# Product of the softmax weights with V as two 64-row halves in two accumulator banks, in bursts of 256 columns, and score maxima 512 wide in a ring of three banks

## The chip, the cores and the metric

The kernel runs on one core of one Trainium2 chip. The metric is the device time of one execution in microseconds (us). The engines of the core work side by side, each through its own list of instructions in order: TensorE (PE in the profile, its weight loads are PEld), VectorE (DVE), ScalarE (ACT), GpSimd (POOL) and SyncE (SP), which here only issues DMAs. TensorE writes its results into PSUM, which has eight banks of 512 fp32 columns on 128 partitions.

## What is computed

```python
def reference(A_x, A_wqkv, A_wo, B_x, B_wqkv, B_wo, gate_w):
    # S = 2048 tokens, D = 512, H = 32 heads of Dh = 16, all fp32; A and B differ in their weights
    def mha(x, wqkv, wo):
        qkv = (x @ wqkv).reshape(B, S, 3, H, Dh).transpose(2, 0, 3, 1, 4)
        q, k, v = qkv[0], qkv[1], qkv[2]
        scores = jnp.einsum("bhqd,bhkd->bhqk", q, k) * (Dh ** -0.5)
        p = softmax(scores, axis=-1)
        o = jnp.einsum("bhqk,bhkd->bhqd", p, v)
        return o.transpose(0, 2, 1, 3).reshape(B, S, D) @ wo
    x = A_x
    g = sigmoid((x * gate_w).sum(-1, keepdims=True))
    return g * mha(x, A_wqkv, A_wo) + (1 - g) * mha(x, B_wqkv, B_wo)
```

There are 64 heads in all, 32 of each side, each with a 2048 by 2048 matrix of scores.

## The kernel before

**Stages.** A prologue computes q, k and v of both sides from the input and stores them in DRAM (`project_qk`, `project_v`); the main loop runs over 64 heads x 16 = 1024 *rounds*, two in each turn; an end finishes the last head and the last output rows. While the main loop runs, heads that are done are divided by their softmax sums and multiplied by `wo` (`load_den`, `invert_den`, `load_num`, `normalize`, `split_out`, `project_out`). Those steps hang on round numbers, in a table that `at(...)` fills.

**A head, three matmuls.** The row maxima are needed before the exponentials, so each score is computed twice. (1) `max_part` (L113) multiplies q by k for 128 queries and 512 keys into `ps_m`, and VectorE takes the maximum over the keys (L125). A tile of 128 queries has 2048 keys: parts 0 and 1 are 512 keys, each in one bank (`ps_m1`, two buffers), and part 2 is 1024 keys in two banks (`ps_m2`, one buffer), so a tile takes three reductions. (2) `score` (L573) multiplies k by q for 128 keys and 512 queries into `ps_st` (three buffers of one bank), with the maxima subtracted by two more contraction rows, and ScalarE takes the exponential into `p` (L585). (3) `attend` (L515) multiplies `p` by v and a column of ones, so that row 16 of 17 is the softmax sum, into the one bank `acc`. The four groups of 512 queries go to four column tiles of the TensorE array (`tile_position=(0, 32 * c)`), each with all 128 rows, and run side by side. `acc` adds over the 16 rounds of a head. Then ScalarE copies it out (L549, `ev`) and a DMA stores it in `od`.

**Rows of the array.** The maxima use 48 contraction rows and the scores 50, at row 0 or row 64 by turns (`rows()`), so two of them run side by side in two row halves with all 128 columns. `attend` uses 128 rows and 32-column tiles. `p` and v are fp32, and each such matmul leaves two records, two passes. The others are fp32r and take one.

**Order.** `tc.manual_schedule()` is on: each engine runs its instructions in the order in which the code issues them. For two rounds the string `FULL` sets it: `e` is a score matmul with its exponential, `m` a part of a maximum tile (`M` the double one), and a digit n is a burst of `attend` over n quarters of 128 query columns. The string is `e3eemm2eMeme3emeM`. Scores run about 2 rounds ahead of `attend`, and maxima 20 rounds ahead of the scores. A `project_out` goes out ahead of a burst. In the prologue `run_ahead` issues the first 20 tiles of maxima, three parts after each `project_v`.

**PSUM.** `ps_m1` two banks, `ps_m2` two, `ps_st` three, `acc` one. A result of `project_out` takes a `ps_m1` buffer.

Of the kernel before, what the change touches and what calls it, by code (L numbers as in the profile page):

```python
# [32 lines left out]
P = 128  # L33
S = 2048
DM = 512
# [16 lines left out]
def gated_mha(ctx: ExitStack, tc: tile.TileContext, xT, x, wqkv_a, wo_a, wqkv_b, wo_b, gate_w, out):  # L52
# [8 lines left out]
    ps_m1 = ctx.enter_context(tc.tile_pool(name="ps_m1", bufs=2, space=PSUM))  # L61
    ps_m2 = ctx.enter_context(tc.tile_pool(name="ps_m2", bufs=1, space=PSUM))
# [4 lines left out]
    od = [dram.tile([HG, NQ, 32, 512], F32, name=f"od{g}") for g in range(2 * NG)]  # L67
# [37 lines left out]
    PARTS = ((0,), (1,), (2, 3))  # L105
# [7 lines left out]
    def max_part(m, part):  # L113
        h, t = divmod(m, NT)
        if t == 0 and part == 0:
            mxp[h] = small.tile([P, NT, 3], F32, name="mxp")
        q, k = q_st[h % 3], k_st[h % 3]
        chunks = PARTS[part]
        n = len(chunks)
        ps = (ps_m1 if n == 1 else ps_m2).tile([P, n * 512], F32, name=f"ps_m{n}")  # L120
        for i, c in enumerate(chunks):
            b = rows()
            pe.matmul(ps[:, i * 512:(i + 1) * 512], q[b:b + SC, t * P:(t + 1) * P],  # L123
                      k[b:b + SC, c * 512:(c + 1) * 512], start=True, stop=True)
        dve.tensor_reduce(mxp[h][:, t, part:part + 1], ps, op=ALU.max, axis=AX.X)  # L125
# [35 lines left out]
    with tc.tile_pool(name="xs", bufs=1) as xs, tc.tile_pool(name="pro", bufs=2) as pro, \  # L161
# [59 lines left out]
        def project_v(s, t):  # L221
            hi, lo = wblocks[s, 2 * DM]
            c, o = divmod(t * P, 512)
            last = s == 1 and t == NT - 1
            ps = ps_m1.tile([P, 512], F32, name="ps_m1") if last else ps_pro.tile([P, 1024], F32, name="ps_pro")
            n = 0
            for a, b in ((xh[c], hi), (xl[c], hi), (xh[c], lo)):
                for k in range(KC):
                    pe.matmul(ps[:, :DM], a[:, k, o:o + P], b[:, k], start=n == 0, stop=n == 3 * KC - 1)  # L229
# [20 lines left out]
        ahead = [(m, part) for m in range(NT + LEAD) for part in range(3)]  # L250

        def run_ahead(n):
            turn[0] = 0
            for _ in range(n):
                m, part = ahead.pop(0)
                max_part(m, part)
                if (m, part) == (NT - 1, 2):
                    max_split(0)
                    pending.append(0)

        pending = []
        for i, (s, g, isk) in enumerate(blocks):
            block(split_w, i + 1)
            block(load_w, i + 3)
            if i in (2, 8):
                load_w(i // 8, 2 * DM, DM)
            if i in (4, 9):
                split_w(i // 8, 2 * DM, DM)
            project_qk(s, g, isk, lambda: run_ahead((i >= 10) + (i >= 13)))
# [27 lines left out]
    acc = ps_acc.tile([P, 512], F32, name="acc")  # L297
    dve.memset(acc, 0.0)
# [60 lines left out]
    def load_den(G):  # L359
        o, n = od[G], gh[G] * DH  # L360
        dens[G] = work.tile([P, P], F32, name="dn")
        nc.sync.dma_start(dens[G][:n], bass.AP(tensor=o.tensor, offset=o.offset + 16 * 512,
                                               ap=[[32 * 512, gh[G] * NQ], [P, 4], [1, P]]))

    def invert_den(G, i):
        n = gh[G] * DH
        if i == 0:
            dens["r", G] = work.tile([P, P], F32, name="rn")
        rn = dens["r", G]
        c = slice(i * 64, i * 64 + 64)  # L370
        dve.reciprocal(rn[:n, c], dens[G][:n, c])  # L371
        if i:
            nc.sync.dma_start(rd[G][:gh[G]].rearrange("h (x e) -> (h x) e", e=P), rn[:n])


    def load_num(G, c):
        o, r, n = od[G], rd[G], gh[G] * DH
        num = work.tile([P, 512], F32, name="o_num", bufs=4)
        rb = work.tile([P, 512], F32, name="rb", bufs=4)
        nc.sync.dma_start(num[:n], bass.AP(tensor=o.tensor, offset=o.offset + c * 32 * 512,  # L380
                                           ap=[[NQ * 32 * 512, gh[G]], [512, DH], [1, 512]]))
# [4 lines left out]
    def normalize(G, c):  # L386
        n = gh[G] * DH
        num, rb = nums[G, c]
        (dve if G == LAST else pool).tensor_tensor(num[:n], num[:n], rb[:n], op=ALU.mult)

    def split_out(G, c, slot):
        n = gh[G] * DH
        num, _ = nums.pop((G, c))
# [7 lines left out]
    def result_bank():  # L401
        banks.append(len(banks) % 5)
        if banks[-1] % 2 or not fill_only:
            return ps_m1.tile([P, 512], F32, name="ps_m1")
# [86 lines left out]
    for side in range(2):  # L491
# [4 lines left out]
        for c in range(NQ):  # L496
            for i, G in enumerate(groups):
                at(end + 22 + 16 * c + i, load_num, G, c)
                at(end + 28 + 16 * c + i, normalize, G, c)
                at(end + 34 + 16 * c + 2 * i, split_out, G, c, i)  # L500
            for i in range(4):
                at(end + 42 + 16 * c + 2 * i, project_out, side, 4 * c + i)
# [5 lines left out]
    for c in range(NQ):  # L508
        at(end + 4 + c // 2, load_num, LAST, c)
        at(end + 10 + c // 2, normalize, LAST, c)  # L510
        at(end + 11 + c // 2, split_out, LAST, c, c)
# [12 lines left out]
    def attend(r, qa, qb):  # L524
# [6 lines left out]
        for c in range(NQ):  # L531
            pe.matmul(acc[32 * c:32 * c + 17, qa * P:qb * P], v[:, 4 * a + c if final else kt, j],  # L532
                      p[:, c * 512 + qa * P:c * 512 + qb * P], start=first and qa == 0, stop=last,
                      tile_position=(0, 32 * c), skip_group_check=True)
# [3 lines left out]
        if final and last:  # L538
            ev = work.tile([P, 512], F32, name="ev")
            dve.tensor_copy(ev, acc)  # L540
# [5 lines left out]
        elif last:  # L546
            G, j = divmod(h, HG)
            ev = work.tile([P, 512], F32, name="ev")
            act.copy(ev, acc)  # L549
            nc.sync.dma_start(od[G][j].rearrange("c r t -> (c r) t"), ev)  # L550
# [15 lines left out]
    def score_bank(r):  # L566
        if r >= ROUNDS - NT - LEAD:
            late[0] += 1
            if late[0] % 6 in (1, 3):
                return ps_m1.tile([P, 512], F32, name="ps_m1")  # L570
            if late[0] % 6 == 5:
                return ps_m2.tile([P, 1024], F32, name="ps_m2")[:, :512]
# [17 lines left out]
    FULL = "e3eemm2eMeme3emeM"  # L590
    after = {}

    for r in range(0, ROUNDS, 2):
# [12 lines left out]
        for step in FULL if m < ROUNDS else ():  # L606
# [3 lines left out]
            elif step in "mM":  # L610
                max_part(m + parts // 3, parts % 3)
# [50 lines left out]
```

## Time and profile before

| | |
|---|---|
| time, two runs | 2849.75 and 2850.84 us, median 2850.3 us |
| profiled execution | span 2848.8 us from the first to the last instruction, granted TensorE clock 0.998; what lies around the span is 1.5 us of the median |
| TensorE busy | 2830.3 us, 99% |
| VectorE busy | 2559.5 us, 90% |
| ScalarE busy | 2260.3 us, 79% |
| GpSimd busy | 225.3 us, 8% |
| DMA | 214.65 MB, 75 GB/s on average |
| maxima reductions, L125 | 3072, 2419.6 us |
| exponentials, L585 | 4056 into `ps_st` tiles, 2157.0 us |

How to read it: matmuls are pipelined and the ends in the records are modelled, so a matmul of 0.4 us may be followed by the next one of its kind 0.23 us later, and a TensorE that is 99% busy is not at its limit for 99% of the time. Records of VectorE overlap in the same way when it works without a gap. What one instruction costs in a row of its kind is read from start to start.

### The profile page before, as it was taken

What the parts mean: (1) busy time and instruction counts of PE and PEld (TensorE: products, weight loads), DVE (VectorE), ACT (ScalarE), POOL (GpSimd) and SP (SyncE); (2) the same over time, 40 slices, a digit from 0 to 9 for tenths busy, and PEclk for the clock granted to TensorE, in tenths of its full rate; (3) what the DMA queues carried; (4) which work ended last, traced back from release to release, by engine and by line L of the source; (5) the groups of instructions that cost most, each with busy time, mean ns of one, the idle gap of its engine ahead of it and who ended that gap; (6) DMA issues with size and microseconds to landing.
All of it is one profiled execution on the core that took longest, in us unless ns stands there. A gap on an engine that the chain in (4) does not pass through costs nothing.

```text
span 2848.8 us, 62282 instructions
## 1 busy us (share of the span) xinstructions
PE 2830.3 (99%) x26016; PEld 1372.6 (48%) x26016; DVE 2559.5 (90%) x3371; ACT 2260.3 (79%) x4253; POOL 225.3 (8%) x369
## 2 busy tenths in 40 slices
PE   8999999999999999999999999999999999999999
PEld 7877444444444444444444455444444444444544
DVE  4135899999999999999999988999999999998894
ACT  3221788889888888988988866888888888987775
POOL 1000232000000000000100231000000000011201
PEclk9999999999999999999999999999999999999999
DMA  7673333222332222332322342232222233323302
GB/s 244 195 230 121 88 80 80 40 49 54 66 58 55 52 56 46 54 56 55 85 55 49 95 101 55 54 56 48 59 47 55 55 74 66 54 67 85 72 10 91
DMA packets 83759, 214.65 MB, mean 75 GB/s; under 512 B 21878, under 2 KB 32086, under 8 KB 70934
## 3 DMA queue, kind: packets, MB, share of 16 engines
q1 hardware_dynamic: 80918, 201.76, 31.1%
q0 software_dynamic: 2560, 8.91, 1.2%
q8 instruction: 205, 3.36, 0.5%
q14 instruction: 76, 0.62, 0.1%
HBM read 145.87 MB, written 64.74 MB: 74 GB/s over the span
## 4 chain that ended last, share of the span: by engine, by line
PE 91%; DVE 7%; DMA 1%; ACT 0%; SPq 0%; issue 0%; POOL 0%; DVEq 0%; ACTq 0%
PE acc L532 34%; PE ps_st L583 29%; PE ps_m L123 14%; DVE mxp L125 7%; PE ps_pro L206 6%; PE ps_m L416 3%; PE ps_pro L229 3%; DMA raw<-in_xT 0%; DMA rb<-rd 0%; PE ps_st L416 0%; DVE rn L371 0%; PE ps_st L467 0%; ACT p L585 0%; PE ps_m L583 0%; PE ps_m L467 0%
## 5 line engine op out<-in xcount | busy, mean ns | idle before, releaser
L125 DVE TENSOR_REDUCE mxp<-ps_m 128x1 f32<-128x512 f32 (+1 forms) x3072 | 2419.6, 861 | 49.8 <-PE ps_m L123 43.5
L585 ACT ACTIVATE p<-ps_st 128x512 f32<-128x512 f32 x4056 | 2157.0, 601 | 332.6 <-PE ps_st L583 233.7
L583 PE MATMUL ps_st<-q_st,k_st 50*128 50x512 f32 x4056 | 1322.9, 445 | 0.0
L123 PE MATMUL ps_m<-k_st,q_st 48*128 48x512 f32 x4096 | 1199.0, 434 | 3.6 <-DVE mxp L125 3.1
L532 PE MATMUL acc<-p,vg 128*17 128x384 f32 (+1 forms) x16208 | 1188.3, 386 | 3.0 <-DVE ev L540 2.0
L583 PEld LDWEIGHTS ps_st<-q_st,k_st 50*128 50x128 f32 x4056 | 591.8, 184 | 745.7 <-ACT p L585 723.8
L123 PEld LDWEIGHTS ps_m<-k_st,q_st 48*128 48x128 f32 x4096 | 543.1, 185 | 105.6 <-DVE mxp L125 39.4
L532 PEld LDWEIGHTS acc<-p,vg 128*17 128x17 f32 x16208 | 314.0, 96 | 512.1 <-issue 481.0
L136 POOL CAST mparts<-mrow 128x16 fp32r<-128x16 f32 x64 | 12.5, 196 | 2194.5 <-DVE mrow L135 2194.5
L211 DVE TENSOR_TENSOR part<-ps_pro,part 128x1024 fp32r<-128x1024 f32 x32 | 39.2, 1225 | 110.5 <-ACT part L210 110.5
L210 ACT CAST part<-ps_pro 128x1024 fp32r<-128x1024 f32 x32 | 32.5, 1015 | 132.0 <-PE ps_pro L206 132.0
L416 PE MATMUL ps_m<-wo,ot 128*128 128x512 f32 (+1 forms) x354 | 90.4, 400 | 0.0
L206 PE MATMUL ps_pro<-xh,whi 128*128 128x512 f32 x256 | 73.2, 405 | 8.0 <-ACT xh L192 7.5
L232 ACT COPY v_st<-ps_pro 128x512 f32<-128x512 f32 x31 | 18.2, 587 | 77.4 <-PE ps_pro L229 77.4
L416 PEld LDWEIGHTS ps_m<-wo,ot 128*128 128x128 f32 (+1 forms) x354 | 64.0, 188 | 23.8 <-DVE mxp L125 8.7
L206 PE MATMUL ps_pro<-xh,wlo 128*128 128x512 f32 x256 | 69.3, 393 | 0.0
L206 PE MATMUL ps_pro<-xl,whi 128*128 128x512 f32 x256 | 69.2, 393 | 0.0
L206 PEld LDWEIGHTS ps_pro<-xh,whi 128*128 128x128 f32 x256 | 47.9, 192 | 23.1 <-ACT xh L192 10.2
L206 PEld LDWEIGHTS ps_pro<-xh,wlo 128*128 128x128 f32 x256 | 48.6, 190 | 10.3
L206 PEld LDWEIGHTS ps_pro<-xl,whi 128*128 128x128 f32 x256 | 48.6, 190 | 10.2
L180 DVE TENSOR_TENSOR wlo<-wraw,whi 128x512 fp32r<-128x512 f32 x16 | 10.9, 684 | 46.8 <-ACT whi L179 46.8
L549 ACT COPY ev<-acc 128x512 f32<-128x512 f32 x63 | 38.2, 607 | 0.0
(92 smaller groups left out, 634.4 us busy)
## 6 DMA issues: line engine op xcount, KB each, us to landing
k_st<-kd SPq DMA_DIRECT2D x128, 256.0 KB
q_st<-qd SPq DMA_DIRECT2D x128, 256.0 KB
qd<-part SPq DMA_DIRECT2D x32, 512.0 KB
kd<-part SPq DMA_DIRECT2D x32, 512.0 KB
k_st<-kd SPq DMA_DIRECT2D x128, 128.0 KB
q_st<-qd SPq DMA_DIRECT2D x128, 128.0 KB
od<-ev SPq DMA_DIRECT2D x63, 256.0 KB
vd<-v_st SPq DMA_DIRECT2D x32, 272.0 KB
```

The lines of the kernel that those rows point to most:

```text
L123: pe.matmul(ps[:, i * 512:(i + 1) * 512], q[b:b + SC, t * P:(t + 1) * P], k[b:b + SC, c * 512:(c + 1) * 512], start=True, stop=True)
L125: dve.tensor_reduce(mxp[h][:, t, part:part + 1], ps, op=ALU.max, axis=AX.X)
L206: pe.matmul(ps[:, c * 512:(c + 1) * 512], a[:, k], b[:, k], start=n == 0, stop=n == 3 * KC - 1)
L210: act.copy(pt[0], ps)
L211: dve.tensor_tensor(pt[1], ps, pt[0].bitcast(F32), op=ALU.subtract)
L229: pe.matmul(ps[:, :DM], a[:, k, o:o + P], b[:, k], start=n == 0, stop=n == 3 * KC - 1)
L232: act.copy(v_st[t % 2][:, :, 0:16], v)
L416: pe.matmul(ps, ot[a][:n, slot, sl], wt[b][:n, g], start=G == groups[0] and i == 0, stop=G == groups[-1] and i == 2)
L532: pe.matmul(acc[32 * c:32 * c + 17, qa * P:qb * P], v[:, 4 * a + c if final else kt, j], p[:, c * 512 + qa * P:c * 512 + qb * P], start=fi ...
L549: act.copy(ev, acc)
L583: pe.matmul(ps, k[b:b + SC + 2, kk * P:(kk + 1) * P], q[b:b + SC + 2, cc * 512:(cc + 1) * 512], start=True, stop=True)
L585: act.activation(pt[r][:, c * 512:(c + 1) * 512], ps, AF.Exp, scale=SCALE)
```

## The change

- `attend` splits each matmul of 128 contraction rows into two of 64 rows (rows 0 to 63 and 64 to 127 of `p` and v), which go to the two row halves of the array and into two accumulator banks, `acc0` and `acc1`. A burst has eight matmuls where it had four.
- At the end of a head ScalarE copies both banks out, and two DMAs store them in two `od` tensors. The sum of the two halves is taken later, where the heads are divided: one more load and one more addition in `normalize` and `invert_den`, and for the last head one more VectorE addition.
- The second accumulator takes a bank from the maxima. `ps_m` is one ring of three banks, and a tile of maxima has four parts of 512 keys: four reductions where there were three.
- `FULL` is `2emem2emem2emem2emem`: four bursts of two quarters (256 columns) for two rounds where there were three of 3, 2 and 3 quarters. `run_ahead` issues four parts after each `project_v`. Results of `project_out` and some scores of the last head use the ring of three.
- The steps that divide and project are moved by some rounds in their table.

```diff
-    ps_m1 = ctx.enter_context(tc.tile_pool(name="ps_m1", bufs=2, space=PSUM))
-    ps_m2 = ctx.enter_context(tc.tile_pool(name="ps_m2", bufs=1, space=PSUM))
+    ps_m = ctx.enter_context(tc.tile_pool(name="ps_m", bufs=3, space=PSUM))
...
     def max_part(m, part):
...
-        chunks = PARTS[part]
-        n = len(chunks)
-        ps = (ps_m1 if n == 1 else ps_m2).tile([P, n * 512], F32, name=f"ps_m{n}")
-        for i, c in enumerate(chunks):
-            b = rows()
-            pe.matmul(ps[:, i * 512:(i + 1) * 512], q[b:b + SC, t * P:(t + 1) * P],
-                      k[b:b + SC, c * 512:(c + 1) * 512], start=True, stop=True)
+        ps = ps_m.tile([P, 512], F32, name="ps_m")
+        b = rows()
+        pe.matmul(ps, q[b:b + SC, t * P:(t + 1) * P], k[b:b + SC, part * 512:(part + 1) * 512],
+                  start=True, stop=True)
         dve.tensor_reduce(mxp[h][:, t, part:part + 1], ps, op=ALU.max, axis=AX.X)
...
             if t and t != NT - 2:
-                run_ahead(3)
+                run_ahead(4)
...
-    acc = ps_acc.tile([P, 512], F32, name="acc")
+    acc = [ps_acc.tile([P, 512], F32, name=f"acc{i}") for i in range(2)]
...
     def normalize(G, c):
-        num, rb = nums[G, c]
-        (dve if G == LAST else pool).tensor_tensor(num[:n], num[:n], rb[:n], op=ALU.mult)
+        (num, more), rb = nums[G, c]
+        eng = dve if G == LAST else pool
+        eng.tensor_tensor(num[:n], num[:n], more[:n], op=ALU.add)
+        eng.tensor_tensor(num[:n], num[:n], rb[:n], op=ALU.mult)
...
     def attend(r, qa, qb):
...
         for c in range(NQ):
-            pe.matmul(acc[32 * c:32 * c + 17, qa * P:qb * P], v[:, 4 * a + c if final else kt, j],
-                      p[:, c * 512 + qa * P:c * 512 + qb * P], start=first and qa == 0, stop=last,
-                      tile_position=(0, 32 * c), skip_group_check=True)
+            for i, b in enumerate(HALVES):
+                pe.matmul(acc[i][32 * c:32 * c + 17, qa * P:qb * P],
+                          v[b:b + 64, 4 * a + c if final else kt, j],
+                          p[b:b + 64, c * 512 + qa * P:c * 512 + qb * P], start=first and qa == 0, stop=last,
+                          tile_position=(b, 32 * c), skip_group_check=True)
...
         if final and last:
-            dve.tensor_copy(ev, acc)
+            dve.tensor_copy(ev, acc[0])
+            dve.tensor_tensor(ev, ev, acc[1], op=ALU.add)
...
         elif last:
-            act.copy(ev, acc)
-            nc.sync.dma_start(od[G][j].rearrange("c r t -> (c r) t"), ev)
+            for i in range(2):
+                ev = work.tile([P, 512], F32, name=f"ev{i}", bufs=1)
+                act.copy(ev, acc[i])
+                nc.sync.dma_start(od[G][i][j].rearrange("c r t -> (c r) t"), ev)
...
-    FULL = "e3eemm2eMeme3emeM"
+    FULL = "2emem2emem2emem2emem"
```

In the main loop TensorE's list reads so before, from one burst of 384 columns to the middle burst and beyond it (`ps_m1` and `ps_m2` are the buffers of maxima, `x4` are the four column tiles):

```order
L532 MATMUL acc_2015<-p_11674,vg_8358 17x384 x4
L583 MATMUL ps_st_11744<-q_st0_113,k_st0_114 128x512
L583 MATMUL ps_st_11747<-q_st0_113,k_st0_114 128x512
L123 MATMUL ps_m1_11750<-k_st1_118,q_st1_117 128x512
L123 MATMUL ps_m1_11753<-k_st1_118,q_st1_117 128x512
L532 MATMUL acc_2015<-p_11674,vg_8358 17x128 x4
L532 MATMUL acc_2015<-p_11709,vg_8358 17x128 x4
L583 MATMUL ps_st_11764<-q_st0_113,k_st0_114 128x512
```

The middle burst crosses from one round's `p` to the next, so its 256 columns are two groups of 128. In the changed kernel the list of the same loop, from the end of one burst to the start of the next, is:

```order
L534 MATMUL acc0_2060<-p_17319,vg_10345 17x256
L534 MATMUL acc1_2061<-p_17319,vg_10345 17x256
L586 MATMUL ps_st_17422<-q_st1_122,k_st1_123 128x512
L118 MATMUL ps_m_17425<-k_st2_2056,q_st2_2055 128x512
L586 MATMUL ps_st_17428<-q_st1_122,k_st1_123 128x512
L118 MATMUL ps_m_17431<-k_st2_2056,q_st2_2055 128x512
L534 MATMUL acc0_2060<-p_17360,vg_10345 17x256
L534 MATMUL acc1_2061<-p_17360,vg_10345 17x256
```

The last two rows are followed by three more pairs, one for each further column tile. Every burst now has eight matmuls in two banks, and between any two bursts stand two scores and two maxima.

In the prologue, TensorE's list around the maxima after one `project_v` (L229) was:

```order
L229 MATMUL ps_pro<-wvlo,xh_133 128x512 x4
L123 MATMUL ps_m_1631<-k_st_114,q_st_113 128x512
L123 MATMUL ps_m_1634<-k_st_114,q_st_113 128x512
L123 MATMUL ps_m_1637<-k_st_114,q_st_113 128x512 x2
L229 MATMUL ps_pro<-wvhi,xh_133 128x512 x4
```

and in the changed kernel, where `project_v` is L224:

```order
L224 MATMUL ps_pro<-wvlo,xh_138 128x512 x4
L118 MATMUL ps_m<-k_st_119,q_st_118 128x512 x4
L224 MATMUL ps_pro<-wvhi,xh_139 128x512 x4
L224 MATMUL ps_pro<-wvhi,xl_143 128x512 x4
L224 MATMUL ps_pro<-wvlo,xh_139 128x512 x4
```

The four maxima matmuls went into four banks, two of them as one buffer. Now they are four tiles of a ring of three.

On ScalarE the end of the first head reads so before (`ev` is the copy of the accumulator; the `x70` and `x64` are the exponentials):

```order
L232 COPY v_st_141<-ps_pro 128x32x16
L232 COPY v_st_142<-ps_m_1967 128x32x16
L585 ACTIVATE p<-ps_st 128x512 x70
L549 COPY ev<-acc 128x512
L585 ACTIVATE p<-ps_st 128x512 x64
```

and in the changed kernel:

```order
L227 COPY v_st_147<-ps_m 128x32x16
L588 ACTIVATE p<-ps_st 128x512 x70
L554 COPY ev_2810<-acc_2060 128x512
L554 COPY ev_2813<-acc_2061 128x512
L588 ACTIVATE p<-ps_st 128x512 x64
```

Two copies stand one behind the other between the same exponentials.

More of the change, by code (lines that the diff above doesn't have):

```diff
@@ L249, in gated_mha @@
                 block(load_w, c)
-        ahead = [(m, part) for m in range(NT + LEAD) for part in range(3)]
+        ahead = [(m, part) for m in range(NT + LEAD) for part in range(NQ)]
         def run_ahead(n):
@@ L568, in score_bank @@
             late[0] += 1
[L569 to L572, printed above, removed]
+            if late[0] % 2:
+                return ps_m.tile([P, 512], F32, name="ps_m")
         return ps_st.tile([P, 512], F32, name="ps_st")
```

62 lines of the change are left out of this document (32 added, 30 removed).

## The prediction

> **What bounds the kernel now.** The page's first part and its chain say TensorE:
>
> ```profile
> PE 2830.3 (99%) x26016; PEld 1372.6 (48%) x26016; DVE 2559.5 (90%) x3371; ACT 2260.3 (79%) x4253; POOL 225.3 (8%) x369
> PE 91%; DVE 7%; DMA 1%; ACT 0%; SPq 0%; issue 0%; POOL 0%; DVEq 0%; ACTq 0%
> ```
>
> But a busy TensorE is not one at its limit, so I read stages next: the table by stretches, first the long parts of the main loop, then one plain head and one in which output rows are projected.
>
> ```profile
> core 0: us, PE busy (x) PEld busy (x) DVE busy (x) ACT busy (x) POOL busy (x), PEclk, DMA share, GB/s
> 340.00:1600.00 1260.00, 1258.79 (x12678) 555.04 (x12680) 1255.90 (x1668) 1129.62 (x2148) 83.93 (x169) 1.00 0.31 60
> 1800.00:2560.00 760.00, 759.45 (x7657) 335.02 (x7660) 757.62 (x1005) 681.38 (x1295) 31.19 (x66) 1.00 0.29 57
> ...
> 836.90:875.00 38.10, 38.10 (x388) 16.85 (x385) 37.99 (x51) 34.29 (x67) 0.42 (x2) 1.00 0.28 52
> 875.00:913.00 38.00, 38.00 (x388) 16.82 (x384) 37.90 (x51) 34.18 (x67) 0.42 (x2) 1.00 0.27 51
> ...
> 1650.40:1700.00 49.60, 49.60 (x435) 25.55 (x432) 41.34 (x56) 34.28 (x67) 13.53 (x16) 1.00 0.35 87
> ```
>
> Over 2020 us of the main loop VectorE is busy for 1255.90 of 1260 and 757.62 of 760 us, 99.7%. A head takes 38.05 us there. Only with `project_out` does it idle (41.34 of 49.60 us), in 8 of the 64 heads. The waits agree: VectorE waits for maxima matmuls 48 times in all, while TensorE's waits for VectorE are short.
>
> ```profile
> DVE mxp L125 <- PE ps_m L123: 43.5, 48, 3.9
> PEld ps_m L123 <- DVE mxp L125: 39.4, 131, 0.9
> PEld acc L532 <- ACT ev L549: 23.6, 63, 1.2
> ```
>
> So **VectorE's reductions set the pace now**, with TensorE close behind. How close is read from single starts. Two rounds of TensorE:
>
> ```profile
> 1500.98 0.84 PE L532 MATMUL acc<-p,vg 128*17 128x384 f32 x8
> 1501.76 0.50 PE L583 MATMUL ps_st<-q_st,k_st 50*128 50x512 f32 x2
> 1502.09 0.39 PE L123 MATMUL ps_m<-k_st,q_st 48*128 48x512 f32 x2
> 1502.41 0.63 PE L532 MATMUL acc<-p,vg 128*17 128x128 f32 x16
> 1502.97 0.50 PE L583 MATMUL ps_st<-q_st,k_st 50*128 50x512 f32 x1
> ...
> 1503.87 0.84 PE L532 MATMUL acc<-p,vg 128*17 128x384 f32 x8
> 1504.64 0.50 PE L583 MATMUL ps_st<-q_st,k_st 50*128 50x512 f32 x1
> ...
> 1505.67 0.52 PE L532 MATMUL acc<-p,vg 128*17 128x384 f32 x4
> ```
>
> A burst of 384 columns holds TensorE 0.77 us until the next kind of matmul begins (1500.98 to 1501.76, 1503.87 to 1504.64), the middle burst of 256 columns 0.56. Two pairs of score and maximum take 0.65 (1501.76 to 1502.41), three pairs 0.90 (1502.97 to 1503.87). Without waits two rounds are 0.77 + 0.65 + 0.56 + 0.90 + 0.77 + 0.90 = 4.55 us; they take 4.69 here, the 0.13 more in the last stretch. VectorE in the same place:
>
> ```profile
> 1500.20 1.28 DVE L125 TENSOR_REDUCE mxp<-ps_m 128x1 f32<-128x512 f32 x2
> 1501.39 1.22 DVE L125 TENSOR_REDUCE mxp<-ps_m 128x1 f32<-128x1024 f32 x1
> 1501.39 1.81 DVE L125 TENSOR_REDUCE mxp<-ps_m 128x1 f32<-128x1024 f32 x2
> ```
>
> Two 512-wide reductions take 1.19 us from start to start of what follows (1500.20 to 1501.39). In the third row a wide one and a narrow one last 1.81; the second row of the pair 1500.20 gives a narrow one's own record as 1.28 - 0.60 = 0.68, so the wide one holds VectorE 1.81 - 0.68 = 1.13. A tile costs 1.19 + 1.13 = 2.32.
>
> **The change, part by part.** *Reductions.* Four narrow ones cost 2 x 1.19 = 2.38 per tile, 0.06 more: a wide reduction of 1024 columns pays its fixed part once. Nothing hides this on an engine that is 99.7% busy, so VectorE alone already needs 16 x 0.06 = 1.0 us more per head, about 39.05 us, if it waits no less than now.
>
> *Bursts.* The columns to stream stay the same; the number of bursts in two rounds goes from three to four. Each end of a burst costs something: 0.77 - 0.56 = 0.21 for 128 columns more in two passes is 0.82 ns per column and pass, so 256 columns stream in 0.42 and 0.14 of the 0.56 is switching. A further 0.15 lies in the stretch of pairs, where the first two take 0.65 and the third adds 0.25. Does switching stay when a burst uses the same row halves as the scores? The trace has no such burst. The nearest rows are a switch in columns alone, from `project_out` (128 rows and 128 columns) to a burst (128 rows, 32-column tiles):
>
> ```profile
> 1628.11 3.04 PE L416 MATMUL ps_m<-wo,ot 128*128 128x512 f32 x12
> 1630.75 0.39 PE L416 MATMUL ps_m<-wo,ot 128*128 128x512 f32 x1
> 1631.07 0.84 PE L532 MATMUL acc<-p,vg 128*17 128x384 f32 x8
> ```
>
> The last of the twelve starts at 1630.75 and the burst 0.32 later. Inside the group eleven steps take 2.64, so 0.24 each. The same rows on both sides thus do not save the switch, about 0.08 to 0.1 us, as much as where rows and columns change (1502.09 plus a pair's 0.25 to 1502.41). Bounds: all of the switching stays (a quarter of the loop is 0.56 + 0.65 = 1.21), or all goes (0.42 + 2 x 0.25 = 0.92). I take the first, to which the column switch is nearest.
>
> [...]
>
> Eight matmuls start where four did, one after another:
>
> ```profile
> 836.77 0.13 PEld L532 LDWEIGHTS acc<-p,vg 128*17 128x17 f32 x8 [0.27 <-issue]
> L532 PEld LDWEIGHTS acc<-p,vg 128*17 128x17 f32 x16208 | 314.0, 96 | 512.1 <-issue 481.0 <-ACT ev L549 23.6 <-ACT p L585 3.9
> ```
>
> Eight weight loads of 0.096 us span 0.13, so their starts lie 5 ns apart; four further tiles delay a burst's end by 0.02 to 0.03. The quarter is then 0.59 + 0.65 = **1.24**, and two rounds **4.96 us**. VectorE needs 4 x 1.19 = 4.76 for them. TensorE becomes the bound, by 0.2.
>
> *The second copy.* At a head's end the next burst waits for both copies of the accumulators. ScalarE's rows at such a place, and the start of an exponential after its score at 1502.97:
>
> ```profile
> 836.91 1.08 ACT L585 ACTIVATE p<-ps_st 128x512 f32<-128x512 f32 x2
> 837.87 0.60 ACT L549 COPY ev<-acc 128x512 f32<-128x512 f32 x1
> 838.33 0.64 ACT L585 ACTIVATE p<-ps_st 128x512 f32<-128x512 f32 x1
> 1503.51 0.60 ACT L585 ACTIVATE p<-ps_st 128x512 f32<-128x512 f32 x1
> ```
>
> Exponentials follow each other by 0.48 (836.91 to 837.87 for two), a copy holds ScalarE 0.46, and an exponential starts 0.54 after its score. Count from the start of a head's last burst. Its two scores stood at -0.65 and -0.32, their exponentials start at -0.11 and 0.37, the copies at 0.85 and 1.31, and the second ends at 1.91 with its record of 0.60. The next burst would start at 1.24; its second matmul writes the second bank. TensorE stands still for about **0.7 us per head**, with scores, maxima and `project_out` queued behind that burst. Bounds: 0.2 (if the first copy alone counts) to 0.9. Now the copy has three pairs of cover ahead of the next burst and one bank; no such stall adds to the 38.05, since VectorE works on through it.
>
> A head then takes 8 x 4.96 + 0.7 = 40.4 us, 2.35 more than 38.05. The string runs for 1004 of the 1024 rounds, 62.75 heads: **147 us**. Heads with `project_out` pay the same: the twelve matmuls (2.96 us to the burst) stand apart from the rest.
>
> *The prologue.* Three parts fitted in four banks; four parts meet three.
>
> ```profile
> 245.13 0.73 PE L123 MATMUL ps_m<-k_st,q_st 48*128 48x512 f32 x4
> 245.79 1.18 PE L229 MATMUL ps_pro<-wvhi,xh 128*128 128x512 f32 x4
> 248.71 0.50 PE L123 MATMUL ps_m<-k_st,q_st 48*128 48x512 f32 x2
> 245.66 2.42 DVE L125 TENSOR_REDUCE mxp<-ps_m 128x1 f32<-128x512 f32 x3 [2.73 <-PE ps_m L123]
> ```
>
> The first reduction starts 0.53 after the first matmul and its record ends 0.69 later, at 1.22. Only then may the fourth matmul start, which stood at 0.34: 0.9 us more for `project_v` behind it, in 14 places, **13 us**. There TensorE sets the pace (3.58 from group to group, of which VectorE fills 2.42), so it is paid in full.
>
> *The rest.* Two DMAs instead of one per head, one more load per numerator and GpSimd's additions lie beside the loop: GpSimd is 8% busy, DMA moves 57 to 60 GB/s there, and a head's numerators have tens of rounds. Without that cover a late numerator would hold `project_out` and TensorE with it, some us in 8 heads. In the last head four chunks of the accumulator get one addition more each on VectorE, at the price of this row of the same size:
>
> ```profile
> L420 DVE TENSOR_SCALAR o_acc<-ps_m,gate 128x512 f32<-128x512 f32 x4 | 3.0, 751 | 5.4 <-PE ps_m L416 5.4
> ```
>
> 4 x 0.75 is **3 us**. The sum is 147 + 13 + 3 = 163 on the execution's span of 2848.8, and with the 1.5 us between this span and the median of 2850.3, **3013; I say 3010 us**, 5.6% slower.
>
> **The rivals.**
> 1. *VectorE stays the bound.* The switching gets cheaper in part (the two row halves drain or load apart), two rounds of TensorE fall below 4.8, and the copies hide in its slack. Then only the 1.0 us per head of the reductions counts: 63 + 13 + 3 on 2850.3 gives 2930. For it: the sum above has TensorE only 0.2 of 4.96 ahead. Against it: the column switch.
> 2. *Not slower: no switching at all.* A quarter is 0.92 and two rounds 3.7, so VectorE never waits: 16 x 2.38 = 38.1 and 0.4 for a head's two small instructions, 38.5, which adds 28 us. After each `project_out` the first maximum starts about 0.7 earlier (burst 0.42 and no pair of scores ahead of it, against 0.77 and 0.33), 32 times, 22 us back. With 16 for the ends: 2875, within 2%. It decides from 4.76 per two rounds downwards. Even here it is not faster, for VectorE's floor has risen.
> 3. *The change doesn't do what it says: the two halves run one after the other.* Each burst then takes 0.42 more, two rounds 6.64, a head 15.8 us more: 3860. Scores and maxima do run side by side in two row halves (two L583 rows in 0.50), and four column tiles do too; eight tiles at once, no row shows.
>
> **How the numbers follow.** Forecast 0.62 (2940 with the short stall of 0.2 and no further tile delay, where VectorE has caught up, to 3045 with 0.9 and 0.3 per head of waits in the ring of three), rival 1 0.17, rival 2 0.12, rival 3 0.06, and 0.03 for what I don't see. About 2% is what a measurement of this kernel can tell from no change, 2793 to 2907. Rival 2 is "same", the rest slower, and 0.02 I leave for faster. The range reaches from 2900, below rival 1, to 3050; it leaves out rivals 2 and 3.
>
> **What would show it.** Reductions all 512 wide, 0.60 from start to start where VectorE has no gap: the first step. Gaps of 0.1 to 0.2 on VectorE in each two rounds and a busy share of about 95% in the loop: TensorE is the bound; 99% and heads of 39: rival 1. A burst of 256 columns that takes 0.59 until the next score, and 0.32 from the last pair to a burst: the switching stayed; 0.42 and 0.25: rival 2. Waits of the accumulator matmuls for the copies near 0.7 x 63 = 44 us more: the second copy. The prediction is wrong above all if the row halves change what a switch costs.

## The result: 3038.8 us, 6.6% slower, with TensorE as the bound

The changed kernel takes 3038.8 us (median of two runs, 3037.64 to 3039.97) against 2850.3 us. The ratio is 1.066, its 95% interval 1.0629 to 1.0691. The forecast was 3010 us in a range of 2900 to 3050. The profiled execution has a span of 3038.2 us, 189.4 more than before.

The page's first part and its chain, after:

```profile
PE 2995.2 (99%) x42224; PEld 1266.6 (42%) x42224; DVE 2688.0 (88%) x4412; ACT 2349.0 (77%) x4316; POOL 261.8 (9%) x397
PE 90%; DVE 5%; ACT 2%; DMA 1%; issue 1%; POOL 0%; SPq 0%; DVEq 0%; POOLq 0%; ACTq 0%
```

These read like those of before (TensorE 99%, 91% of the chain), though the bound is another one now. What tells is the loop. ScalarE's copies of the accumulators mark the heads: two plain neighbours, and the first and the last copy (the last row of each kernel is that of its last copies; the columns are count, least, median and greatest ns, then the first start and the last).

```profile
894.72 1.08 ACT L554 COPY ev<-acc 128x512 f32<-128x512 f32 x2
935.28 1.08 ACT L554 COPY ev<-acc 128x512 f32<-128x512 f32 x2
...
L554 ACT COPY ev<-acc x2: 592/604/616, 365.0 to 365.4; 128x512 f32<-128x512 f32 x2
...
L554 ACT COPY ev<-acc x2: 767/779/791, 2965.8 to 2966.2; 128x512 f32<-128x512 f32 x2
```

The same of before:

```profile
L549 ACT COPY ev<-acc x1: 604/604/604, 341.2 to 341.2; 128x512 f32<-128x512 f32 x1
...
L549 ACT COPY ev<-acc x1: 766/766/766, 2785.2 to 2785.2; 128x512 f32<-128x512 f32 x1
```

A plain head takes 40.56 us here (935.28 - 894.72; the median over all heads is 40.59) against 38.05. From the first copy to the last lie 62 heads: 2965.8 - 365.0 = 2600.8 us against 2785.2 - 341.2 = 2444.0. So the 189.4 us split into **23.8 before the first copy, 156.7 in the loop and 8.9 after the last copy** (3038.2 - 2965.8 = 72.4 against 63.6, to rounding). The copy rows of the second kernel also show one cause at once: 1.08 us for two copies, where one of 0.60 stood.

Inside the loop, TensorE after (start, duration, what):

```profile
1502.01 0.65 PE L534 MATMUL acc<-p,vg 64*17 64x256 f32 x16
1502.59 0.50 PE L586 MATMUL ps_st<-q_st,k_st 50*128 50x512 f32 x1
...
1502.92 0.39 PE L586 MATMUL ps_st<-q_st,k_st 50*128 50x512 f32 x1
...
1503.25 0.65 PE L534 MATMUL acc<-p,vg 64*17 64x256 f32 x16
```

The sixteen matmul records of a burst fit in one row of 0.65 us, so the two row halves do run side by side (rival 3 is out). The burst holds TensorE 0.58 until the next score, the two pairs 0.66 until the next burst, and a quarter takes 1503.25 - 1502.01 = **1.24 us, as forecast** (the median of some 600 between 900 and 1640 us is 1.243). From the last pair to the burst pass 0.33 (1502.92 to 1503.25): the switch between row halves with all columns and row halves with 32 columns costs what the switches of before cost (0.32 from the last pair to the burst). What TensorE does in that time these rows do not show; what rival 1 says of the two row halves is a supposition.

VectorE's reductions as a group (busy time, mean ns of one, and the idle time before them), and the loop in the table by stretches:

```profile
L120 DVE TENSOR_REDUCE mxp<-ps_m 128x1 f32<-128x512 f32 x4096 | 2540.6, 685 | 87.6 <-PE ps_m L118 81.8
...
340.00:1700.00 1360.00, 1354.07 (x21380) 504.47 (x21378) 1335.92 (x2226) 1189.22 (x2205) 83.64 (x174) 1.00 0.31 63
```

VectorE's share of the loop is 98% (1335.92 of 1360), yet it has slack. A reduction's own record is 0.685 us long, while one that follows without a wait starts 0.60 after the one before it. Here 64 of them share a head of 40.59, one in 0.63, so the records overlap and hide the slack. The forecast of visible gaps and of 95% was wrong for that; the slack itself the experiments show.

A head's end:

```profile
934.44 0.65 PE L534 MATMUL acc<-p,vg 64*17 64x256 f32 x16
935.02 0.49 PE L586 MATMUL ps_st<-q_st,k_st 50*128 50x512 f32 x1
...
935.93 1.14 PE L534 MATMUL acc<-p,vg 64*17 64x256 f32 x16 [0.18 <-ACT ev L554]
...
936.41 0.15 PEld L534 LDWEIGHTS acc<-p,vg 64*17 64x17 f32 x14 [0.38 <-ACT ev L554]
936.99 0.49 PE L586 MATMUL ps_st<-q_st,k_st 50*128 50x512 f32 x1
```

The last burst of a head starts at 934.44, and its score stands at 935.02, so without a wait the next burst's score would stand at 936.26. The burst's first matmul waits for the first copy (935.28 + 0.60), the others for the second, and the score comes at 936.99: a stall of **0.73 us**, 0.7 forecast. Then 32 x 1.243 + 0.73 = 40.5 is the head, but for 0.08.

The waits in full, to be set beside those of before:

```profile
PEld acc L534 <- ACT ev L554: 55.0, 110, 1.2
PE acc L534 <- ACT ev L554: 10.1, 55, 0.7
PEld ps_m L118 <- DVE mxp L120: 24.2, 38, 1.5
```

Accumulator matmuls wait 55.0 us for copies where they waited 23.6. TensorE's waits for VectorE's maxima fell from 39.4 us in 131 places to 24.2 in 38, and 17.3 of the 24.2 lie before the loop (up to 320 us): VectorE no longer holds TensorE in plain heads. It still does in every eighth head, where it also prepares a division: 41.54 us against 40.59 (before the change 38.79 against 38.05).

In the prologue TensorE shows the ring of three:

```profile
299.63 1.19 PE L224 MATMUL ps_pro<-wvhi,xh 128*128 128x512 f32 x4
...
302.58 0.73 PE L118 MATMUL ps_m<-k_st,q_st 48*128 48x512 f32 x3
303.86 0.49 PE L118 MATMUL ps_m<-k_st,q_st 48*128 48x512 f32 x1 [0.55 <-DVE mxp L120]
304.28 1.20 PE L224 MATMUL ps_pro<-wvhi,xh 128*128 128x512 f32 x4
```

The fourth maximum starts 1.28 after the first, and a step takes 4.65 us (299.63 to 304.28) where it took 3.58.

At the start of the loop the granted clock (third column from the right) drops:

```profile
312.00:342.00 30.00, 28.55 (x291) 9.50 (x291) 22.36 (x37) 18.05 (x33) 3.10 (x3) 0.66 0.45 84
```

Before, the same place had:

```profile
290.00:320.00 30.00, 28.18 (x213) 13.40 (x211) 23.37 (x30) 19.37 (x37) 4.88 (x3) 0.89 0.47 106
```

In pieces of 10 us the clock reads 1.00 from 300 to 310 us, 0.50 from 320 to 330 and 1.00 from 340 on, so I count with these two values alone, an estimate. Then a mean of 0.66 over 30 us is half clock for 2 x 0.34 x 30 = 20.4 us, against 2 x 0.11 x 30 = 6.6. Two bursts in the half-clock stretch:

```profile
317.81 1.08 PE L534 MATMUL acc<-p,vg 64*17 64x256 f32 x16
...
319.97 1.08 PE L534 MATMUL acc<-p,vg 64*17 64x256 f32 x16
```

A quarter takes 2.16 us there in place of 1.24, so 0.43 of the time is lost: (20.4 - 6.6) x 0.43, **about 6 us of the 23.8** (an estimate). The other run of the changed kernel had a mean clock of 0.997 against 0.995 here and a span 2.3 us shorter, so part of this belongs to the profiled execution.

### The profile page after: what moved, and what is told of

Its sections match the earlier page's. It is cut to its first block, busy times and chain, and to the rows that moved or that the text cites. A ratio compares the mean times of both kernels' runs of the same rounds, so it can differ in the third digit from the quotient of the medians.

```text
span 3038.2 us, 95993 instructions
## 1 busy us (share of the span) xinstructions
PE 2995.2 (99%) x42224; PEld 1266.6 (42%) x42224; DVE 2688.0 (88%) x4412; ACT 2349.0 (77%) x4316; POOL 261.8 (9%) x397
## 4 chain that ended last, share of the span: by engine, by line
PE 90%; DVE 5%; ACT 2%; DMA 1%; issue 1%; POOL 0%; SPq 0%; DVEq 0%; POOLq 0%; ACTq 0%
PE ps_st L586 38%; PE acc L534 37%; PE ps_pro L201 5%; DVE mxp L120 4%; PE ps_m L417 3%; PE ps_pro L224 3%; PE ps_m L118 3%; ACT p L588 1%; ACT ev L554 1%; DMA raw<-in_xT 0%; DMA md<-mt 0%; DMA rb<-rd 0%; PE ps_st L417 0%; PE ps_m L586 0%; PE ps_st L468 0%
## 5 line engine op out<-in xcount | busy, mean ns | idle before, releaser
L120 DVE TENSOR_REDUCE mxp<-ps_m 128x1 f32<-128x512 f32 x4096 | 2540.6, 685 | 87.6 <-PE ps_m L118 81.8
L588 ACT ACTIVATE p<-ps_st 128x512 f32<-128x512 f32 x4056 | 2211.7, 597 | 409.8 <-PE ps_m L118 341.7
L118 PE MATMUL ps_m<-k_st,q_st 48*128 48x512 f32 x4096 | 1504.1, 448 | 9.3 <-DVE mxp L120 8.3
L586 PE MATMUL ps_st<-q_st,k_st 50*128 50x512 f32 x4056 | 1484.6, 445 | 0.7 <-DMA q_st<-md 0.7
L534 PE MATMUL acc<-p,vg 64*17 64x256 f32 x32416 | 1364.2, 385 | 18.1 <-ACT ev L554 10.1
L586 PEld LDWEIGHTS ps_st<-q_st,k_st 50*128 50x128 f32 x4056 | 599.5, 185 | 854.6 <-ACT p L588 818.1
L534 PEld LDWEIGHTS acc<-p,vg 64*17 64x17 f32 x32416 | 323.2, 92 | 767.6 <-issue 697.8
L118 PEld LDWEIGHTS ps_m<-k_st,q_st 48*128 48x128 f32 x4096 | 619.2, 185 | 34.2 <-DVE mxp L120 24.2
L554 ACT COPY ev<-acc 128x512 f32<-128x512 f32 x126 | 68.3, 607 | 0.0
```

What stands on the lines that cost most here:

```text
L118: pe.matmul(ps, q[b:b + SC, t * P:(t + 1) * P], k[b:b + SC, part * 512:(part + 1) * 512], start=True, stop=True)
L534: pe.matmul(acc[i][32 * c:32 * c + 17, qa * P:qb * P], v[b:b + 64, 4 * a + c if final else kt, j], p[b:b + 64, c * 512 + qa * P:c * 512 + ...
L554: act.copy(ev, acc[i])
L586: pe.matmul(ps, k[b:b + SC + 2, kk * P:(kk + 1) * P], q[b:b + SC + 2, cc * 512:(cc + 1) * 512], start=True, stop=True)
L588: act.activation(pt[r][:, c * 512:(c + 1) * 512], ps, AF.Exp, scale=SCALE)
```

## The experiments

Theory T: TensorE has become the bound, by the fourth burst and the stall behind the second copy. Its rival R: the reductions with their ring of three banks set the pace, and TensorE only waits for them. ScalarE is no third candidate: 64 exponentials at 0.48 us and two copies hold it for less than 32 of the 40.59 us. Ratios, with their 95% intervals, are against the kernel before on the same chip, 2850.8 to 2851.1 us there; heads are the median from copy to copy.

**Reductions alone, with four banks, and with three.** The kernel before, its maxima all 512 wide, one accumulator, three bursts as before (with three banks one bank stays unused). `max_part` and the other uses of the ring are as in the changed kernel and are left out here:

```diff
-    ps_m1 = ctx.enter_context(tc.tile_pool(name="ps_m1", bufs=2, space=PSUM))
-    ps_m2 = ctx.enter_context(tc.tile_pool(name="ps_m2", bufs=1, space=PSUM))
+    ps_m = ctx.enter_context(tc.tile_pool(name="ps_m", bufs=4, space=PSUM))   # bufs=3 in the other
...
-    FULL = "e3eemm2eMeme3emeM"
+    FULL = "e3eemm2emmeme3ememm"
```

> The kernel before with one part of the change alone: maxima 512 wide, four reductions per tile, in a ring of four banks; one accumulator, 128-row bursts of 3, 2 and 3 quarters. Theory T (TensorE takes over in the changed kernel, by its fourth burst and the stall behind the second copy; the reductions cost only their fixed part): VectorE stays the bound and pays 0.06 us per tile, 1.0 us per head on 38.03, so about 39.1 per plain head and 2850 + 65 = 2915 us. Rival R (most of the loss of 188 us is the fourth reduction and the ring of the maxima): 2980 us or more already here or with the ring of three.

> As the run with a ring of four banks, but with a ring of three (one bank stays unused). T: in the loop as the ring of four, 39.1 us per plain head or up to 0.5 more for waits; in the prologue 0.95 us more in 14 places, as in the changed kernel; so 2930 to 2960 us. R: VectorE starves with three banks, plain heads of 40 us and more, 2990 us or more.

With four banks: 2883.7 us, ratio 1.0118 (1.0103 to 1.0133), a head of 38.61. With three: 3060.7 us, 1.0739 (1.0723 to 1.0755), a head of 41.04. The stretch of 800 us in the loop and the waits, with four and then with three:

```profile
840.00:1640.00 800.00, 797.51 (x7936) 319.02 (x7934) 799.31 (x1370) 707.90 (x1345) 34.18 (x68) 1.00 0.31 61
```

```profile
840.00:1640.00 800.00, 784.36 (x7472) 309.85 (x7468) 778.07 (x1290) 670.26 (x1267) 22.38 (x56) 1.00 0.28 53
...
PEld ps_m L119 <- DVE mxp L121: 381.4, 1040, 1.0
DVE mxp L121 <- PE ps_m L119: 76.7, 155, 4.9
```

With four banks VectorE is busy for 799.31 of 800 us and needs 0.56 us more per head, not the 1.0 that was forecast: 64 reductions at 0.60 and 0.35 for a head's small instructions give 38.6, so the 38.05 of before held some 0.4 us of VectorE's own waits, which the ring of four took away. (The records agree: before, the step from a narrow reduction to a wide one takes 0.617 us on average, where narrow ones without a wait follow by 0.598, both between 900 and 1640 us.) So T's 39.1 and 2915 us were too high as well. With three banks and uneven bursts both starve: TensorE waits 381.4 us for reductions, in 1040 places. T had expected 2930 to 2960 here and missed; R's number was right. The ring of three is dear, then, but in this order of steps.

**The same ring with the new order, one accumulator:**

```diff
-    FULL = "e3eemm2emmeme3ememm"
+    FULL = "2emem2emem2emem2emem"
```

> As the run with a ring of three banks, and with the order of the changed kernel too (four bursts of two quarters, two pairs between them), but still one accumulator, 128 rows and one copy per head. T: TensorE needs 4 x (0.56 + 0.65) = 4.84 us in two rounds, 38.7 per head and a short stall behind one copy (0.25): level with VectorE's 39.1, so heads of 39.1 to 39.4 and 2930 to 2950 us; the step from here to the changed kernel (64-row halves: 8 tiles instead of 4, second copy) is then the larger half of the loss, about 90 to 110 us. Rival R2 (the fourth burst as such costs the loss): heads of 40.2 and more, 3000 us or more.

2955.3 us, 1.0371 (1.0356 to 1.0387): 105 us faster than the same ring with three bursts, a little above the 2930 to 2950 that T expected and far below R2's 3000. TensorE at a head's end, one ScalarE row and one wait:

```profile
913.00 0.59 ACT L545 COPY ev<-acc 128x512 f32<-128x512 f32 x1
913.65 0.63 PE L528 MATMUL acc<-p,vg 128*17 128x256 f32 x8 [0.20 <-ACT ev L545]
914.21 0.50 PE L579 MATMUL ps_st<-q_st,k_st 50*128 50x512 f32 x1
914.87 0.63 PE L528 MATMUL acc<-p,vg 128*17 128x256 f32 x8
...
PEld ps_m L119 <- DVE mxp L121: 22.7, 40, 1.0
```

The waits for reductions are nearly gone (22.7 us, from 381.4). The burst of four tiles holds TensorE 0.56 and a quarter 1.22, so 32 quarters are 39.0; with the single copy's stall (0.27 by the same count as above) that is 39.3 of the head's 39.46. So four short bursts pay for switches, and of the orders tried with three banks they are the one that makes the ring bearable. The steps from before to after are now priced: **33 us for narrow reductions, 72 for four bursts on three banks, 84 for the halves and the second copy** (90 to 110 expected). Of the last, 67 lie between the first copy and the last. A plain head grows there by 1.13 us: 0.46 for the second copy (0.73 - 0.27), and the rest, 0.67, fits the later end of eight tiles (a burst of 0.58 against 0.56, 32 times). No run has the halves without the second copy, so this last split rests on the rows alone.

**The second copy on VectorE:**

```diff
-                act.copy(ev, acc[i])
+                (dve.tensor_copy if i else act.copy)(ev, acc[i])
```

> The changed kernel with the copy of the second accumulator on VectorE instead of ScalarE, so that both copies run side by side. T: the stall of TensorE at a head's end falls from 0.73 us to about 0.3, while VectorE (39.9 busy of 40.6 us per head) gains 0.7 of work; heads go from 40.58 to about 40.1 and the time from 3039 to about 3010 us. Rival (VectorE is the true bound of the changed kernel): each head gets 0.6 longer, 3075 us.

3030.0 us, 1.0633 (1.0615 to 1.065), a head of 40.46. By R this adds 0.6 us to each head, for VectorE has more to do. The head became 0.13 shorter. The 0.5 less that T expected did not come, because the copy waits its turn behind reductions: it starts 0.27 after the first where it started 0.48 after, and lasts 0.68 where it lasted 0.60, so it ends 0.13 earlier.

```profile
928.56 0.59 ACT L554 COPY ev<-acc 128x512 f32<-128x512 f32 x1
928.83 0.68 DVE L554 COPY ev<-acc 128x512 f32<-128x512 f32 x1
929.20 1.01 PE L534 MATMUL acc<-p,vg 64*17 64x256 f32 x16 [0.17 <-ACT ev L554]
```

**Half of each reduction, before and after.** Both leave out half of the columns of each maximum (the maximum is taken over half of the keys only), so VectorE gets much less to do and TensorE the same:

```diff
-        dve.tensor_reduce(mxp[h][:, t, part:part + 1], ps, op=ALU.max, axis=AX.X)
+        dve.tensor_reduce(mxp[h][:, t, part:part + 1], ps[:, :256], op=ALU.max, axis=AX.X)   # before: :n * 256
```

> The kernel before with each maximum taken over the first half of its columns only (256 of 512, 512 of 1024; the maxima are then not those of all keys), so VectorE's work in the loop is about halved and nothing else changes. Theory T (VectorE set the pace before): plain heads fall from 38.03 to TensorE's own 8 x 4.55 = 36.4 us plus at most 0.3 for the wait for the copy, and the time to 2740 to 2770 us. Rival (TensorE set it): no more than 10 us.

> The changed kernel with each maximum over the first 256 of its 512 columns (maxima not of all keys). T (TensorE sets the pace after the change): plain heads stay at 40.5 +- 0.1; in the prologue the wait for the ring of three shrinks by about 0.3 in 14 places; 3020 to 3035 us in all. Rival R (the four reductions and their ring are the bound of the changed kernel): heads of 39 us and less, below 2970 us.

Before: 2781.7 us, 0.9753 (0.9738 to 0.9768), a head of 37.08. After: 3017.3 us, 1.0583 (1.0567 to 1.0599), a head of 40.50. The loop and VectorE's wait, of before and then of after:

```profile
840.00:1640.00 800.00, 800.00 (x8174) 378.08 (x8176) 502.94 (x1068) 721.25 (x1373) 50.22 (x87) 1.00 0.32 63
```

```profile
840.00:1640.00 800.00, 796.52 (x12642) 288.62 (x12640) 487.39 (x1313) 703.44 (x1304) 21.77 (x56) 1.00 0.30 60
...
DVE mxp L120 <- PE ps_m L118: 946.8, 1837, 5.7
```

This is the test that tells T and R apart. With VectorE at 61% of the loop (487.39 of 800) the changed kernel's head is 0.09 us shorter, and VectorE waits for TensorE in 1837 places: T holds. (The 21 us that the whole kernel gains: 9 lie before the first copy, where a step of the prologue is 0.27 shorter in 14 places and the half-clock stretch is shorter too, 0.77 over 30 us against 0.66. The rest comes from the 0.09 and from the heads in which VectorE prepares a division, which took 41.5 and now take 40.5 too.) The kernel before gets 0.97 us per head faster in the same test: there VectorE did set the pace, with TensorE's own floor at 37.1. That floor lies above the 36.4 to 36.7 expected, and the time above the 2740 to 2770: two rounds took 4.58 us where they stood at 4.55 in the sum, and some places take longer. With VectorE relieved in both kernels, a head goes from 37.08 to 40.50, which is what the change costs on TensorE's side.

**A second copy that doesn't wait for its bank.** It copies the first copy again, so half of each sum is lost; ScalarE's work stays:

```diff
-                act.copy(ev, acc[i])
+                act.copy(ev, first_ev if i else acc[i])
+                first_ev = ev
```

> The changed kernel with the second copy at a head's end reading the first copy in SBUF instead of the second accumulator (so half of each sum is lost), with ScalarE's work the same: TensorE's next burst then waits for one copy alone. T: the stall at a head's end falls from 0.73 to 0.25 us, plain heads from 40.58 to 40.1, the time by 30 us to about 3009. Rival (the stall is hidden by the slack of another engine): unchanged, 3039.

3027.8 us, 1.0629 (1.0609 to 1.0649), a head of 40.44: 0.15 less, where T expected 0.5. The end of a head:

```profile
927.50 0.62 ACT L554 COPY ev<-ev 128x512 f32<-128x512 f32 x1
927.52 0.65 PE L534 MATMUL acc<-p,vg 64*17 64x256 f32 x16 [0.17 <-ACT ev L554]
928.02 1.56 ACT L589 ACTIVATE p<-ps_st 128x512 f32<-128x512 f32 x3
928.10 0.50 PE L587 MATMUL ps_st<-q_st,k_st 50*128 50x512 f32 x1
928.66 0.49 PE L587 MATMUL ps_st<-q_st,k_st 50*128 50x512 f32 x1
```

The burst goes early now and isn't split. But its two scores stand 0.56 apart instead of 0.33 (928.10, 928.66): ScalarE's two copies delay its exponentials, and with them the score's buffer. The wait has moved. So the second copy is dear as time on ScalarE, not only as a bank that comes free late.

**Eight bursts of 128 columns** (a single run):

```diff
-    FULL = "2emem2emem2emem2emem"
+    FULL = "1em1em1em1em1em1em1em1em"
```

> The changed kernel with eight bursts of one quarter (128 columns) in two rounds and one pair of score and maximum between them: the same matmul columns, but twice as many switches between burst and scores. T: a burst takes 0.015 + 0.046 + 2 x 0.108 + 0.09 = 0.37, a pair with its switch 0.10 + 0.21 + 0.11 = 0.42, two rounds 8 x 0.79 = 6.3 us instead of 4.97, a head 50.6 + 0.7 = 51.3, about 3710 us. If 64-row bursts switched for nothing (rival), two rounds would stay below 5.0 and the time near 3040.

5370 us, a head of 84.2. By the sum of switches it was to be 3710. An eighth of two rounds, the loop by stretches, and the page's clock in 40 slices:

```profile
1500.53 0.65 PE L534 MATMUL acc<-p,vg 64*17 64x128 f32 x16
...
1501.83 0.44 PE L534 MATMUL acc<-p,vg 64*17 64x128 f32 x8
...
1000.00:1050.00 50.00, 50.00 (x686) 17.73 (x686) 27.59 (x43) 22.69 (x38) 0.42 (x2) 0.50 0.02 4
...
PEclk9965555555555555555555559999555555555699
```

The clock stood at half for most of the run (0.602 is the mean). It rose to full in the stretch with `project_out` (the four 9s in the middle) and stayed there for four heads after it. Those four, with no `project_out` in them, took 52.1 to 53.8 us, near the 51.3 expected. So the price of switches was judged well as a sum (its single terms are estimates of the author that no run shows apart), and the rest is the clock's: at half clock an eighth takes 1.30 (1500.53 to 1501.83), 83 us for the 64 of a head. The clock is at half without a gap in TensorE's records: from 1000 to 1050 us they fill 50.00 of 50 us while the clock reads 0.50. What brings the clock down these runs do not show.

**Wide reductions in both halves of a tile** (two double banks, each filled by two matmuls that are issued singly), to save VectorE's time without the second accumulator, in two orders:

```diff
-    ps_m1 = ctx.enter_context(tc.tile_pool(name="ps_m1", bufs=2, space=PSUM))
-    ps_m2 = ctx.enter_context(tc.tile_pool(name="ps_m2", bufs=1, space=PSUM))
+    ps_m = ctx.enter_context(tc.tile_pool(name="ps_m", bufs=2, space=PSUM))   # tiles of 1024 columns
...
-    FULL = "e3eemm2eMeme3emeM"
+    FULL = "e3eemm2emmeme3ememm"     # the first
+    FULL = "3emme2emmeemme3emme"     # the second
```

> A try at a version that beats both: the kernel before with two reductions of 1024 columns per tile, in two buffers of two banks, and bursts of 3, 2 and 3 quarters; the halves of a wide buffer are filled one by one in the order of the narrow parts. T (VectorE sets the pace before, its price per tile is 2 x 1.13 = 2.26 instead of 2.32): VectorE's floor falls to 36.2 + 0.4 = 36.6 us per head, but a buffer is filled only when the reduction two before it is done, and from the starts read in the kernel before I count a wait of 0.3 on TensorE and of 0.5 on VectorE in each two rounds, 4.85 us, 38.8 per head: 2880 to 2920 us. If the ring does not bind: heads of 37.1 (what halved reductions gave), 2785 us.

> As the run with two wide buffers, with an order that fills a wide buffer by one pair of matmuls between two scores: 3 quarters, then score, two maxima, score; 2 quarters, then that twice; 3 quarters, then it once. TensorE needs 4.55 us in two rounds, and the fourth score of the middle stretch waits for its bank, about 0.3: 4.85, heads of 38.8, 2880 to 2920 us; if that wait is hidden, heads of 37.1 and 2785 us.

Both expectations failed: 3165.4 us, 1.1098 (1.1079 to 1.1116), and 3006.5 us, 1.0545 (1.053 to 1.0561). The first one's waits:

```profile
PEld ps_m L123 <- DVE mxp L126: 423.8, 504, 1.6
DVE mxp L126 <- PE ps_m L123: 320.9, 455, 4.0
```

TensorE waits for a double buffer to come free and VectorE for its second half, by turns. In the second order TensorE's loads wait 91.3 us for reductions, and yet a head takes 40.44; where the rest goes is left open. Few buffers cost more here than long reductions save. No kernel here that leaves nothing out beats the one before.

**The accumulators zeroed by ScalarE instead of VectorE** (a single run), since the half clock at the loop's start lies behind that zeroing (it starts at 313.08 us in the changed kernel, and from 315 to 320 us the clock reads 0.55):

```diff
-        dve.memset(a, 0.0)
+        act.activation(a, v_st[0].rearrange("p h d -> p (h d)")[:, :512], AF.Copy, scale=0.0)
```

> The changed kernel with the two accumulators zeroed at the loop's start by ScalarE instead of VectorE, where the zeroing stood ahead of reductions and TensorE stood still for 1.66 us before its granted clock fell to 0.5 for 20 us. If that stop is what brings the clock down, the half-clock stretch at the loop's start gets shorter (to some 7 us, as in the kernel before) and the first heads end 5 to 8 us earlier, about 3032 us. If the clock falls anyway, only the 1 us of zeroing is gained.

```profile
312.00:342.00 30.00, 29.52 (x393) 10.44 (x393) 27.78 (x46) 23.85 (x44) 3.13 (x3) 0.89 0.45 85
...
L554 ACT COPY ev<-acc x2: 593/606/619, 358.4 to 358.9; 128x512 f32<-128x512 f32 x2
```

The mean clock of 0.89 is, by the count used above, half clock for 6.6 us, and the first copy came at 358.4, 6.6 us earlier, close to the 6 estimated above. But the run with the second copy on VectorE, with the zeroing where it was, had 0.83 in the same 30 us and its first copy at 360.2. And this run gave some of the time back behind its last copy, 74.7 us against 72.4, where the clock was lower than in the changed kernel (this run, then the changed kernel): 3036.5 us in all.

```profile
2960.00:3030.00 70.00, 61.05 (x442) 30.22 (x440) 37.57 (x62) 31.22 (x63) 10.69 (x12) 0.90 0.26 96
```

```profile
2960.00:3030.00 70.00, 61.33 (x482) 28.63 (x480) 34.59 (x56) 36.82 (x75) 10.71 (x12) 0.95 0.26 95
```

So the length of such a stretch differs between runs of kernels that are alike there; that the zeroing sets it is not shown.

## Why the prediction was right

- **The bound before, VectorE: shown.** Halved reductions make the kernel before 2.5% faster, and no more: TensorE stands at 37.1.
- **TensorE takes over: shown** by the same edit in the changed kernel. A quarter is 1.24 as forecast, the stall 0.73 against 0.7, a head 40.59 against 40.4. Of the missing 0.2, half is the quarter (32 x 0.003 = 0.1), the other half is left open. Heads with `project_out` pay about the same, as forecast. What the forecast did not have: every eighth head, where VectorE prepares a division, is still held by VectorE and pays 2.75 (41.54 against 38.79). Over 62 heads this is 157 against 146, the first 11 us of the error.
- **Reductions: the direction right, the term mis-sized.** Alone they cost 0.56 us per head, not 1.0, since the forecast took VectorE's 38.05 for a floor without waits. That it did no harm in the sum is luck of a kind: the term is covered by TensorE's there; it would have put rival 1 at about 2900 instead of 2930.
- **The switch stays: shown** for the case that the trace of before lacked, with 0.33 us from the last pair to the burst against 0.32. That ruled out rival 2.
- **The second copy: its size right, its reason half right.** The prediction let the burst wait for a bank. Without that wait most of the stall comes back through ScalarE's late exponentials.
- **The prologue: 15, forecast 13.** A step grew by 1.07, not 0.9, in 14 places: the fourth maximum starts 0.94 later, and the matmul behind it another 0.1.
- **The start of the loop: not foreseen, about 6 us** of half clock by the estimate above. The other 3 of the 23.8 (15 + 6 + 3) lie elsewhere before the first copy and are not taken apart.
- **The end: 8.9, forecast 3.** A longer half-clock stretch near the end (0.95 over 70 us here, 0.93 over 23 us before: by the same count 7 us at half clock against 3) and the part of the last head behind the last copy are in it; it is not taken apart further.
- **Waits and shares as signs.** Waits of the accumulators rose by 31 us and 10 more on the matmuls themselves, 44 forecast. VectorE's share of 95% was the sign that failed: 98%, since its records overlap.

The sum was 26 us short of the 189 (163): 11 in the loop, 10 at the start and 5 at the end (the parts of the first and the last head outside the copies counted there). No step that the forecast rests on failed. Missing were the half clock at the start and most of what came at the end; the size of the reductions and VectorE's 95% were wrong, and neither enters the time.

## What to carry to other kernels

Where two engines stand within a few per cent of each other, count both per round from start to start; a change that takes a buffer from one and adds a switch to the other can move the bound, as here from VectorE to TensorE. Slack that the first engine then has is worth little: halved reductions took 0.09 us off a head of 40.59. Whether an engine is the bound is settled not by its busy share, 98% here with slack, but by halving its work. And a buffer ring and the order of issue are one choice: narrow reductions cost 33 us with four banks and uneven bursts, 210 with three banks and the same bursts, and 105 with three banks and even ones.

## What the runs showed of the hardware

- With bursts of 128 columns between single pairs the granted clock read 0.50 from 1000 to 1150, from 2000 to 2100 and from 2960 to 3100 us, and TensorE's records filled 99.99 of the 100 us from 2000; the same kernel with 256 columns read 1.00 from 340 to 1700 us. By the price of 0.82 ns per column and pass and a pair's 0.25 (both estimates of the prediction), streaming would fill 0.46 of an eighth's 0.81 us at full clock (52.1 / 64), 57%, and 0.92 of a quarter's 1.243, 74%. Whether such a share has to do with the clock no run shows.
- Two 64-row halves in eight tiles run as one burst, at 0.02 us more than four tiles of 128 rows (0.58 against 0.56).
- A 512-wide reduction has a record of 0.68 us but a pace of 0.60. An engine that runs at a pace between the two, such as the 0.63 here, has slack and shows hardly any (98% busy).
